# A clustered-attention and MLP kernel: listed times of the code copies, one part's copies on other engines, and a new list of due times

## The chip, the cores and the metric

The kernel runs on one core of a Trainium2 chip. The metric is the device time of one execution in microseconds. The kernel before took 302.92 us as the median of three runs (302.88 to 303.65). A separate, profiled execution took 302.2 us, of which 300.4 us lie between the first and the last instruction (the span); all positions in the trace count from the start of that span.

## The reference

The input holds queries, keys and values for 4 batches, 8 heads, 768 positions and a head width of 64, and 16 cluster centres for each head. Each query and each key is assigned to the centre it is most similar to, and a query sees only the keys of its own cluster:

```
q_assign = np.argmax(np.einsum('bhsd,hcd->bhsc', q_n, c_n), axis=-1)
k_assign = np.argmax(np.einsum('bhsd,hcd->bhsc', k_n, c_n), axis=-1)
mask = q_assign[:, :, :, None] == k_assign[:, :, None, :]
scores = np.where(mask, scale * q @ k.T, -1e9)
attn = softmax(scores);  x = attn @ v
h = x @ w_in                                  # 3072 x 512 by 512 x 2048
out = (h * (1.0 / (1.0 + np.exp(-h)))) @ w_out  # 3072 x 2048 by 2048 x 512
```

## The kernel before, in words

**Stages.** The unit of preparation is a *part*: the tiles of 128 positions of one pair of heads, or of one head. A part is split into a high and a low half-precision piece (`hi` on line 545 and `lo` on line 556, tile `hl`), turned so that the head width lies on the partitions (tile `ab`), and multiplied with the centres (logits). The largest logit is found, and a one-hot code of the cluster is made (`oh`), turned in blocks of 32 by VectorE (`flip`, line 770, tile `ohT`), and copied into 16 further rows of `ab`. These are the *code copies*, `put` on line 780: always four for a part, one for each 32 positions of a tile. The scores matmul (line 861) then runs over 80 rows, so that the code adds a large number where the clusters agree. ScalarE takes the exponential (line 868, tile `P`), TensorE multiplies with the values (line 889), VectorE divides by the sum (`norm`, line 906, tile `xn`), and the result is turned into `xt`. The MLP multiplies `xt` with `w_in` (line 967), gates with a tanh (lines 973 and 978), multiplies with `w_out` (line 1002) and copies the sums out of PSUM (lines 1015 and 1017).

**Loops.** Batch 0 is done in two rounds, positions of tiles 0 and 1 first and of tiles 2 to 5 second, so that the MLP can begin early. In round 0 the parts hold keys and the first two tiles of queries; in round 1 there is one part for each of the four pairs of heads with the four remaining query tiles of both heads (8 tiles in all). Batches 1 to 3 then go through with one part of 12 tiles for each head. In batch 0 the transposes are made by TensorE and the code is scaled while it is copied (the code says `blocks`; lines 790 and 794). In batches 1 to 3 the transposes are DMAs and the copy is a plain one (lines 788 and 792).

**The planner.** Every piece of work is a *step* with an engine, a listed time in nanoseconds, the steps it follows, the buffers it takes and a *key*. The class `Plan` (line 35) runs through these steps once when the program is built. Of all steps whose predecessors and buffers allow it, it takes the one that its listed times let start first; between several that could start at the same moment the lowest key decides. What comes out is a fixed order of instructions for each engine. On the chip each engine keeps that order and waits, by semaphores, for what it needs. So a listed time costs nothing by itself: it decides who stands behind whom. Where TensorE has nothing to do early on, the planner inserts matmuls that no one reads (line 369). The planner also keeps account of a port that VectorE and GpSimd share (line 150).

**Keys.** `AT` holds the due times of the rounds and batches of attention, `ML` those of the ten pieces of MLP work. `LEADS` says how far ahead of its head a part is due (first, second and third entry: round 0, round 1, later batches). Each step in a part adds to the part's key a multiple of a twentieth of the lead (`span`): `hi` none, the copies 13 times. `norm` has the key of its head plus the length of a head less 3.

**Where parts are let go.** `REST` gives, for each pair, the head of round 0 whose first exponential must be listed before the round 1 part of that pair may begin (line 1083). `TS` gives the engines of the four copies of each round 1 part (P is GpSimd, D is VectorE, A is ScalarE), `TQ` those of round 0, `PUTB` those of batches 1 to 3 (one VectorE, three GpSimd). `TR` and `HR` give the engines of the PSUM copy and of `hi` in the round 1 parts.

The listed time of a copy of `n` tiles, with `act_w(m) = 112 + 0.714 m`, `pool_w(m) = 110 + m` and `dve_w(m, r, c) = c + r m`, is on line 796; line 798 makes the step.

Of the kernel before, what the change touches and what calls it, by code (L numbers as in the profile page):

```python
# [34 lines left out]
class Plan:  # L35
# [18 lines left out]
    def step(self, eng, w, fn, after=(), use=(), key=0.0, load=None, hold=0.0, pace=None, flip=False, lag=None, slack=0.0, port=None):  # L54
        s = Step()
        s.eng, s.w, s.fn, s.key, s.load, s.hold, s.flip = eng, w, fn, key, load, hold, flip
        s.lag = self.LAG.get(eng, 0) if lag is None else lag
        s.slack = slack
        s.port = eng == "POOL" if port is None else port
        s.use = list(use)  # L60
        s.n = len(self.steps)
        flat = []

        def gather(a):
            if isinstance(a, (list, tuple)):
                for x in a:
                    gather(x)
            elif a is not None:
                flat.append(a)

        gather(list(after))
        gather(pace)
        s.after = list({id(x): x for x in flat}.values())
        s.start = s.end = None
        for b in s.use:
            b.left += 1
        self.steps.append(s)
        return s
# [130 lines left out]
def kernel(  # L209
# [80 lines left out]
    def buf(name):  # L290
        return Buf(pools[name])
# [4 lines left out]
    def act_w(n):  # L296
        return 112 + 0.714 * n

    def dve_w(n, r=1.05, c=65):
        return c + r * n  # L300

    def pool_w(n, r=1.0):
        return 110 + r * n
# [11 lines left out]
    FLIP = 1800  # L315
    DONE = 0
    WSL = 1000
    AT = [-179.6, -158.1, 86.3, 263.5, 510.0, 780.3]
    ML = [-346.1, 272.3, -79.5, 273.8, 532.7, 887.5, 180.9, 687.8, 766.8, 1323.5]
    PUTB = ["DVE", "POOL", "POOL", "POOL"]  # L320
    VC = ["ACT", "ACT", "POOL", "POOL"]
    VB = "POOL"
# [1 line left out]
    TQ = ["PPPP", "ACT", "PPPA", "PPPA", "PPPP"]  # L324
    TF = ["", "ACT"]
    TR = ["DVE", "ACT", "DVE", "DVE"]
    TS = ["PPPD", "PPPP", "PPPP", "PPPD"]
    RT = ["PE", "PE", "PE", "PE"]
    HI = ["POOL", "POOL", "ACT", "POOL"]
    HR = ["POOL", "DVE", "DVE", "DVE"]  # L330
    LEADS = [931.4, 795.2, 77.1]
    REST = [7, 2, 4, 5]
    RLOAD = [4, 0, 0, 3]
    SOON = [9, 5, 8, 4]
    XT = ["ACT", "DVE", "DVE", "ACT"]
# [159 lines left out]
    def part(b, p, segs, a0, due, lead=20.0, hi_eng="POOL", turn="DMA", twin=False, sub="POOL", code_eng=None, pace=None, wait=None):  # L495
# [3 lines left out]
        n = sum(j1 - j0 for _, _, j0, j1 in segs)  # L499
# [8 lines left out]
        blocks = turn != "DMA" and turn[1] not in ("ACT", "DVE")  # L508
# [17 lines left out]
        for kind, h, j0, j1, t, hs in merged:  # L526
# [35 lines left out]
            w = {"ACT": 100 + 54 * m, "DVE": dve_w(64 * m, 0.55), "POOL": pool_w(64 * m)}[hi_eng]  # L562
# [13 lines left out]
        elif blocks:  # L576
            turned = []
            for c0 in range(0, n, 8):
# [19 lines left out]
                w = act_w(128 * (c1 - c0)) + 60 if turn[0] == "ACT" else dve_w(128 * (c1 - c0), 0.55, 40)  # L598
                turned.append(step(turn[0], w, settle, after=[x], use=[bank, A], key=key + 3 * span))
        else:  # L600
# [12 lines left out]
            def turn_of(c, bank, c0, c1):  # L613
                def turn_pe():
                    pt = banks[bank.i].bitcast(f16)
                    for i, t in enumerate(c):
                        nc.tensor.transpose(
                            pt[0 : c1 - c0, i * 128 : (i + 1) * 128], tiles_of(hl)[:, t, c0:c1], ident
                        )

                return turn_pe

            def settle_of(c, bank, rows_, dst, eng):
                def settle():
                    pt = banks[bank.i].bitcast(f16)[0:rows_, 0 : len(c) * 128]
                    out_ = dst()[0:rows_, where[c[0]] : where[c[0]] + len(c), :].rearrange("p n c -> p (n c)")
                    if rows_ < 128 and eng == "ACT":
                        nc.scalar.activation(out=out_, in_=pt, func=AF.Copy, bias=0.0, scale=gain[0:rows_])
                    elif rows_ < 128:
                        nc.vector.tensor_scalar(out=out_, in0=pt, scalar1=gain[0:rows_], scalar2=None, op0=ALU.mult)  # L630
                    elif eng == "ACT":
                        nc.scalar.copy(out_, pt)
                    else:
                        nc.vector.tensor_copy(out_, pt)

                return settle

            def settle_w(c, eng):
                return act_w(128 * len(c)) + 60 if eng == "ACT" else dve_w(128 * len(c), 0.55, 40)
# [126 lines left out]
        if turn == "DMA" or blocks:  # L766
            puts = [{"P": "POOL", "D": "DVE", "A": "ACT"}[e] for e in turn[1]] if blocks else code_eng
            gain_ = OHV if blocks else 1.0

            def flip():  # L770
                nc.vector.transpose(  # L771
                    T["ohT"][ohT.i][:, 0:n, :].rearrange("p n c -> p (n c)"),
                    T["oh"][oh.i][:, 0:n, :].rearrange("p n c -> p (n c)"),
                )

            s_flip = step("DVE", dve_w(32 * n, 1.04, 95), flip, after=marks, use=[oh, ohT], key=key + 12 * span)
            placed = []
            for g in range(4):

                def put(g=g):  # L780
                    dst = T["ab"][A.i][64 : 64 + HC, a0 : a0 + n, 32 * g : 32 * g + 32]
                    src = T["ohT"][ohT.i][32 * g : 32 * g + HC, 0:n, :]
                    if puts[g] == "SP":
                        nc.sync.dma_start(dst, src)
                    elif puts[g] == "ACT":
                        nc.scalar.activation(out=dst, in_=src, func=AF.Copy, bias=0.0, scale=gain_)
                    elif puts[g] == "POOL" and not blocks:
                        nc.gpsimd.tensor_copy(dst, src)  # L788
                    elif puts[g] == "POOL":
                        nc.gpsimd.tensor_scalar(out=dst, in0=src, scalar1=gain_, scalar2=1.0, op0=ALU.mult, op1=ALU.mult)  # L790
                    elif not blocks:
                        nc.vector.tensor_copy(dst, src)
                    else:
                        nc.vector.tensor_scalar(out=dst, in0=src, scalar1=gain_, scalar2=None, op0=ALU.mult)

                w = {"ACT": 200 + act_w(32 * n) * 0.75, "POOL": pool_w(32 * n) + (85 if blocks else 0), "DVE": dve_w(32 * n, 0.08, 255), "SP": 600}[puts[g]]
                load = 10 * n if puts[g] == "SP" else None
                placed.append(step(puts[g], w, put, after=[s_flip, s_log], use=[ohT, A], key=key + 13 * span, load=load, port=puts[g] == "DVE", lag=Plan.LAG.get(puts[g], 0) + DONE))

        else:  # L800
            last = {}
            for c in chunks:
                bank = buf("M")
                x = step("PE", 57 * len(c), turn_of(c, bank, D, HW), after=[marks, his, s_ident], use=[hl, bank], key=key + 12 * span)
                x = step(
                    turn[1], settle_w(c, turn[1]) + (50 if turn[1] == "DVE" else 0),
                    settle_of(c, bank, HW - D, lambda: T["ab"][A.i][:, a0 : a0 + n, :], turn[1]),
                    after=[x], use=[bank, A], key=key + 13 * span,
                )
                for t in c:  # L810
                    last[t] = x
# [235 lines left out]

    want = {(n, h): AT[n] + (AT[n + 1] - AT[n]) * h / H for n in range(NU + B - 1) for h in range(H)}

# [14 lines left out]
    for h in range(2):  # L1064
        part(
            0, 0, [("k", h, 0, NJ), ("q", h, 0, NA)], (NJ + NA) * h, want[0, h], lead=LEADS[0], hi_eng=HI[0],
            turn=(TK[h], TQ[h], TF[h]), wait=s_split if h else None, **engines,
        )
    for p in range(1, NP):
        part(  # L1070
            0, p, [("k", 0, 0, NJ), ("k", 1, 0, NJ), ("q", 0, 0, NA), ("q", 1, 0, NA)], 0, want[0, 2 * p], lead=LEADS[0],
            hi_eng=HI[p], turn=(TK[1 + p], TQ[1 + p]), wait=s_cent, **engines,
# [4 lines left out]
    def at(place, f):  # L1077
        todo.setdefault(place, []).append(f)

    for p in range(NP):  # L1080
        at(RLOAD[p], lambda s, p=p: load_q(0, p, want[1, 2 * p] - 30, NA, NJ, pace=s))
        at(
            REST[p],
            lambda s, p=p: part(
                0, p, [("q", 0, NA, NJ), ("q", 1, NA, NJ)], 2 * (NJ + NA), want[1, 2 * p], lead=LEADS[1], pace=s,
                hi_eng=HR[p], **(engines | dict(turn=(TR[p], TS[p])) if RT[p] == "PE" else dict(code_eng=PUTB)),
            ),
        )
    for b in range(1, B):
        for p in range(NP):  # L1090
# [5 lines left out]
            for i in range(2):  # L1096
                at(
                    place + i - (SOON[2] if soon else SOON[3]),
                    lambda s, b=b, p=p, i=i: part(
                        b, p, [("k", i, 0, NJ), ("q", i, 0, NJ)], 12 * i, want[b + NU - 1, 2 * p + i], lead=LEADS[2], pace=s, code_eng=PUTB  # L1100
                    ),
                )
    for place in range(H * (B + NU - 1)):
        n, h = divmod(place, H)
        per = (AT[n + 1] - AT[n]) / H
        if n < NU:
# [12 lines left out]
    for n, (b, j0, j1) in enumerate(units):  # L1119
        mlp(b, j0, j1, ML[n], ML[n + 1], lambda t, n=n: EVAC[n], n == len(units) - 1)  # L1120

# [31 lines left out]
```

## Time and profile before

| what | before |
|---|---|
| median of three runs | 302.92 us |
| lowest and highest run | 302.88 and 303.65 us |
| profiled execution | 302.2 us |
| its span | 300.4 us |
| granted TensorE clock | 1.000 |
| busy TensorE matmul | 293.8 us (98%) |
| busy ScalarE | 224.7 us (75%) |
| busy VectorE | 206.5 us (69%) |
| busy GpSimd | 126.3 us (42%) |

How to read it: PE is the matmul side of TensorE, PEld its weight loads, DVE is VectorE, ACT is ScalarE, POOL is GpSimd and SP the engine that issues most DMAs. A group of instructions is given as line, engine, operation, output and inputs, shapes and count; then the busy time of the group in us, the mean duration in ns, and the idle time of the engine just before these instructions with what ended it. A row of the timeline gives the start in us, the duration in us, the engine and the group. Matmuls are pipelined: the record of one overlaps that of the next, so busy time on PE hides short gaps.

### The profile page before, as it was taken

The numbers are of one execution on the slowest core, as the hardware profiler recorded it, in microseconds if no ns is written. First come the engines' busy times: TensorE is split into PE (matmuls) and PEld (weight loads), VectorE is DVE, ScalarE is ACT, GpSimd is POOL, SyncE is SP. The second block draws the span as 40 slices with busy tenths as digits, with TensorE's granted clock in tenths as the row PEclk, the third lists the DMA queues.
The fourth block names the chain that finished last, engine by engine and source line by source line (L and its number), as shares of the span: only waits on it lengthen the run. The fifth ranks groups of instructions, "written<-read, shape, count | busy, mean of one in ns | idle before, by whom it ended". The sixth has DMA issues, their size and how long they took to land.

```text
span 300.4 us, 8210 instructions
## 1 busy us (share of the span) xinstructions
PE 293.8 (98%) x3170; PEld 192.0 (64%) x3170; DVE 206.5 (69%) x504; ACT 224.7 (75%) x464; POOL 126.3 (42%) x253
## 2 busy tenths in 40 slices
PE   8899999999999999999999999999999999999996
PEld 6797776678677674666666665666676555555543
DVE  6879876759998894799878794677662343453342
ACT  2999999987899994899889874798898543563120
POOL 6789892645648474455765630232321000000000
PEclk9999999999999999999999999999999999999999
DMA  7999499993699989539798790052111210020212
GB/s 223 267 264 331 86 185 228 143 312 108 99 158 248 248 218 222 195 71 219 129 256 196 185 250 16 35 116 55 27 38 28 62 37 0 0 107 37 100 38 72
DMA packets 71095, 42.12 MB, mean 140 GB/s; under 512 B 50448, under 2 KB 68112, under 8 KB 71056
## 3 DMA queue, kind: packets, MB, share of 16 engines
q1 hardware_dynamic: 66352, 37.23, 49.0%
q0 software_dynamic: 4288, 4.20, 9.6%
q8 instruction: 25, 0.41, 0.5%
q10 hardware_dynamic: 416, 0.16, 0.2%
q14 instruction: 14, 0.11, 0.1%
HBM read 27.30 MB, written 6.29 MB: 112 GB/s over the span
## 4 chain that ended last, share of the span: by engine, by line
PE 87%; ACT 4%; DMA 3%; DVE 2%; POOL 2%; issue 1%; SPq 0%; POOLq 0%; ACTq 0%; DVEq 0%
PE bank L1002 28%; PE bank L967 26%; PE bank L861 19%; PE bank L889 10%; DMA nk<-in_k_dram 3%; ACT P L868 2%; PE bank L676 2%; POOL ab L790 1%; ACT tn L973 1%; PE bank L584 1%; PE bank L369 0%; DVE xn L907 0%; PE bank L667 0%; POOL hl L554 0%; PE bank L671 0%
## 5 line engine op out<-in xcount | busy, mean ns | idle before, releaser
L868 ACT ACTIVATE P<-bank 128x512 f16<-128x512 f32 x288 | 156.5, 640 | 10.2 <-PE bank L861 9.4
L1002 PE MATMUL bank<-wout_s,gq 128*128 128x512 f16 (+2 forms) x400 | 97.3, 371 | 0.0
L967 PE MATMUL bank<-xt,win_s 128*128 128x384 f16 (+1 forms) x576 | 95.2, 308 | 0.1
L973 ACT ACTIVATE tn<-bank 128x384 f32<-128x384 f32 (+1 forms) x144 | 66.6, 487 | 36.8 <-PE bank L967 32.8
L978 DVE SCALAR_TENSOR_TENSOR gq<-tn,bank 128x384 f16<-128x384 f32 (+1 forms) x144 | 69.4, 501 | 33.9 <-ACT tn L973 30.4
L861 PE MATMUL bank<-ab 80*128 80x256 f16 (+1 forms) x384 | 88.1, 326 | 1.9 <-POOL ab L790 1.2
L967 PEld LDWEIGHTS <-win_s 128*128 128x128 f16 x576 | 54.9, 97 | 27.6 <-issue 0.4
L1002 PEld LDWEIGHTS <-gq 128*128 128x128 f16 x400 | 37.6, 98 | 33.7
L788 POOL COPY ab<-ohT 16x384 f16<-16x384 f16 x72 | 38.2, 530 | 33.5 <-DVE ohT L771 16.4
L861 PEld LDWEIGHTS <-ab 80*128 80x128 f16 x384 | 34.8, 97 | 25.2 <-issue 1.7
L889 PEld LDWEIGHTS <-P 128*128 128x128 f16 x1152 | 44.3, 97 | 9.9
L889 PE MATMUL bank<-vt,P 128*128 128x65 f16 x1152 | 47.6, 193 | 0.0
L726 POOL TENSOR_TENSOR Df<-L,mx 128x192 f32<-128x192 f32 x24 | 13.8, 576 | 48.2 <-DVE mx L714 48.0
L558 DVE SCALAR_TENSOR_TENSOR hl<-nk,hl 128x384 f16<-128x384 f32 (+1 forms) x29 | 22.0, 759 | 4.7 <-POOL hl L554 4.5
L558 DVE SCALAR_TENSOR_TENSOR hl<-nq,hl 128x384 f16<-128x384 f32 (+3 forms) x33 | 22.2, 672 | 2.3 <-POOL hl L554 2.3
L1017 DVE COPY ot<-bank 128x512 f32<-128x512 f32 (+2 forms) x14 | 9.1, 648 | 16.1 <-PE bank L1002 16.1
L907 DVE TENSOR_TENSOR xn<-bank,rz 128x384 f16<-128x384 f32 (+2 forms) x40 | 18.7, 472 | 0.8
L694 DVE TENSOR_REDUCE L<-bank 128x192 f32<-128x384 f32 x24 | 13.2, 550 | 7.9 <-PE bank L676 7.6
L771 DVE STREAM_TRANSPOSE ohT<-oh 128x384 f16<-128x384 f16 (+2 forms) x32 | 18.1, 566 | 0.6
L433 POOL CAST vt<-nv 128x384 f16<-128x384 f32 x28 | 16.7, 625 | 3.9 <-DMA nv<-in_v_dram 3.7
L554 POOL TENSOR_SCALAR hl<-nk 128x384 f16<-128x384 f32 (+1 forms) x28 | 15.7, 560 | 2.7 <-DMA nk<-in_k_dram 1.9
L790 POOL TENSOR_SCALAR ab<-ohT 16x256 f16<-16x256 f16 (+1 forms) x28 | 15.7, 561 | 2.5 <-DVE ohT L771 0.6
(68 smaller groups left out, 181.1 us busy)
## 6 DMA issues: line engine op xcount, KB each, us to landing
nv<-in_v_dram SPq DMA_DIRECT2D x16, 384.0 KB, 5.2
out_dram<-ot SPq DMA_DIRECT2D x23, 256.0 KB, 2.1
nk<-in_k_dram SPq DMA_DIRECT2D x15, 384.0 KB, 4.6
nq<-in_q_dram SPq DMA_DIRECT2D x12, 384.0 KB, 4.3
win_s<-in_moe_w_in_dram POOLq DMA_DIRECT2D x4, 512.0 KB, 5.9
wout_s<-in_moe_w_out_dram POOLq DMA_DIRECT2D x8, 256.0 KB, 6.1
nq<-in_q_dram SPq DMA_DIRECT2D x4, 256.0 KB, 6.0
nk<-in_k_dram SPq DMA_DIRECT2D x2, 192.0 KB, 2.7
```

What stands on the lines that cost most here:

```text
L558: nc.vector.scalar_tensor_tensor(out=dl, in0=src, scalar=qs, in1=dh, op0=ALU.mult, op1=ALU.subtract)
L771: nc.vector.transpose(T["ohT"][ohT.i][:, 0:n, :].rearrange("p n c -> p (n c)"), T["oh"][oh.i][:, 0:n, :].rearrange("p n c -> p (n c)"),)
L788: nc.gpsimd.tensor_copy(dst, src)
L790: nc.gpsimd.tensor_scalar(out=dst, in0=src, scalar1=gain_, scalar2=1.0, op0=ALU.mult, op1=ALU.mult)
L861: nc.tensor.matmul(banks[sb.i][:, at : at + 128 * (c1 - c0)], ab[0:80, kt[j], :], ab[0:80, qt + c0 : qt + c1, :].rearrange("p n c -> p (n ...
L868: nc.scalar.activation(out=T["P"][P.i][:, 0:at], in_=banks[sb.i][:, 0:at], func=AF.Exp, bias=0.0, scale=ESC if b else -ESC)
L889: nc.tensor.matmul(banks[O.i][:, (D + 1) * t : (D + 1) * t + nn], w, vt[:, VW * j : VW * j + nn], start=(j == 0), stop=(j == NJ - 1), skip ...
L907: nc.vector.tensor_tensor(out=T["xn"][xn.i][:, 0:nq, (h % 2) * D : (h % 2) * D + D], in0=banks[O.i][:, 0 : (D + 1) * nq].rearrange("p (t c ...
L967: nc.tensor.matmul(banks[bank.i][:, 0:n], win_s[:, r, ts(fb, 128)], T["xt"][xtb[b].i][:, r, 128 * j0 : 128 * j1], start=(r == 0), stop=(r ...
L973: nc.scalar.activation(out=T["tn"][tn.i][:, 0:n], in_=banks[bank.i][:, 0:n], func=AF.Tanh, bias=0.0, scale=1.0)
L978: nc.vector.scalar_tensor_tensor(out=T["gq"][g.i][:, fb % 4, 0:n], in0=T["tn"][tn.i][:, 0:n], scalar=1.0, in1=banks[bank.i][:, 0:n], op0=A ...
L1002: nc.tensor.matmul(banks[bank.i][:, 0 : c1 - c0], T["gq"][gqs[fc // 4].i][:, fc % 4, ts(t, 128)], wout_s[:, fc, c0:c1], start=(fc == 0), s ...
```

## The change

The listed times of a code copy on ScalarE and on GpSimd are replaced by straight lines of their own; VectorE's stays. One more copy of the round 1 part of the last pair goes to VectorE (`PPPD` becomes `PDPD`). The round 1 part of the third pair is let go at head 3 in place of head 4 (`REST`). All due times and leads get new values. No instruction is added or removed; one of the 28 scaled copies of GpSimd becomes one of VectorE. Everything else is the order that the planner makes from these numbers.

```diff
-    AT = [-179.6, -158.1, 86.3, 263.5, 510.0, 780.3]
-    ML = [-346.1, 272.3, -79.5, 273.8, 532.7, 887.5, 180.9, 687.8, 766.8, 1323.5]
+    AT = [-183.7, -157.7, 95.1, 260.4, 516.1, 766.8]
+    ML = [-353.6, 275.4, -77.4, 274.9, 528.1, 885.0, 180.6, 698.2, 763.6, 1320.2]
...
-    TS = ["PPPD", "PPPP", "PPPP", "PPPD"]
+    TS = ["PPPD", "PPPP", "PPPP", "PDPD"]
...
-    LEADS = [931.4, 795.2, 77.1]
-    REST = [7, 2, 4, 5]
+    LEADS = [931.2, 800.6, 77.5]
+    REST = [7, 2, 3, 5]
...
-                w = {"ACT": 200 + act_w(32 * n) * 0.75, "POOL": pool_w(32 * n) + (85 if blocks else 0), "DVE": dve_w(32 * n, 0.08, 255), "SP": 600}[puts[g]]
+                w = {"ACT": 222 + 27 * n, "POOL": 215 + 30 * n if blocks else 50 + pool_w(32 * n), "DVE": dve_w(32 * n, 0.08, 255), "SP": 600}[puts[g]]
```

## The prediction

> **What bounds the kernel now.** The page's head comes first: the busy times and, in its fourth part, the chain of work that ended last.
>
> ```profile
> span 300.4 us, 8210 instructions
> ...
> PE 293.8 (98%) x3170; PEld 192.0 (64%) x3170; DVE 206.5 (69%) x504; ACT 224.7 (75%) x464; POOL 126.3 (42%) x253
> ...
> PE 87%; ACT 4%; DMA 3%; DVE 2%; POOL 2%; issue 1%; SPq 0%; POOLq 0%; ACTq 0%; DVEq 0%
> ```
>
> TensorE holds 87% of the chain, so the end moves only by what TensorE waits for. Busy time in stretches says where that is; the cut at 35.88 us is the first MLP matmul in the chain.
>
> ```profile
> 0.00:35.88 35.88, 32.97 (x548) 27.43 (x549) 29.63 (x90) 30.09 (x54) 28.96 (x70) 1.00 0.87 235
> 35.88:60.00 24.12, 24.12 (x294) 16.68 (x293) 16.99 (x46) 23.80 (x55) 15.65 (x33) 1.00 1.16 186
> 60.00:236.00 176.00, 175.23 (x1972) 115.12 (x1969) 133.88 (x324) 150.05 (x314) 81.67 (x153) 1.00 0.63 148
> 236.00:297.50 61.50, 61.49 (x369) 32.73 (x366) 25.73 (x46) 20.80 (x42) 0.00 (x0) 1.00 0.13 47
> ```
>
> The columns are the length, then PE, PEld, DVE, ACT and POOL busy, the clock and the DMA share. From 35.88 to 297.5 us TensorE is idle for 0.00 + 0.77 + 0.01 = 0.78 us. So everything the change can win lies in the first 36 us or in a few holes of the middle. The group of matmuls that no one reads belongs to the first part:
>
> ```profile
> L369 PE MATMUL bank<-zeros 128*128 128x256 f16 x59 | 10.1, 319 | 1.0 <-DVE zeros L347 1.0
> ```
>
> 10.1 of the 32.97 us at the start are such filling. There, TensorE waits for the other engines, and between 20 and 36 us all of these are full:
>
> ```profile
> 20.00:30.00 10.00, 9.66 (x191) 8.36 (x189) 9.11 (x27) 10.00 (x20) 9.18 (x16) 1.00 1.09 317
> 30.00:36.00 6.00, 5.63 (x96) 4.01 (x95) 5.45 (x20) 5.61 (x13) 5.30 (x13) 1.00 0.24 57
> ```
>
> **The listed times.** The groups of code copies, shapes kept apart:
>
> ```profile
> L788 POOL COPY ab<-ohT 16x384 f16<-16x384 f16 x72 | 38.2, 530 | 33.5 <-DVE ohT L771 16.4 <-PE bank L861 6.9 <-PE bank L676 2.1
> L790 POOL TENSOR_SCALAR ab<-ohT 16x256 f16<-16x256 f16 x18 | 8.9, 497 | 1.3 <-ACT P L868 0.2
> ...
> L790 POOL TENSOR_SCALAR ab<-ohT 16x512 f16<-16x512 f16 x10 | 6.8, 677 | 1.2 <-DVE ohT L771 0.6
> L786 ACT ACTIVATE ab<-ohT 16x512 f16<-16x512 f16 x2 | 1.2, 625 | 0.0
> L794 DVE TENSOR_SCALAR ab<-ohT 16x256 f16<-16x256 f16 x2 | 0.8, 410 | 0.1
> ```
>
> Line 796 worked out: the plain copy of 12 tiles (384 elements) goes from 110 + 384 = 494 to 50 + 494 = 544 ns (measured 530), the scaled one of 16 tiles from 707 to 695 (677), of 8 tiles from 451 to 455 (497), ScalarE's of 16 tiles from 558 to 654 (625). By itself this adds no nanosecond. It matters where the plan believed GpSimd early and put VectorE behind it. TensorE's holes after 35.88 us come from that engine. The first, in the timeline:
>
> ```profile
> 79.53 1.04 POOL L788 COPY ab<-ohT 16x384 f16<-16x384 f16 x2
> ...
> 81.21 0.84 DVE L558 SCALAR_TENSOR_TENSOR hl<-nk,hl 128x384 f16<-128x384 f32 x1 [0.30 <-POOL hl L554]
> ...
> 81.37 1.03 PE L861 MATMUL bank<-ab 80*128 80x512 f16 x5
> ...
> 82.19 0.56 DVE L907 TENSOR_TENSOR xn<-bank,rz 128x384 f16<-128x384 f32 x1
> ...
> 82.81 0.38 PE L861 MATMUL bank<-ab 80*128 80x256 f16 x2 [0.40 <-DVE xn L907]
> ```
>
> GpSimd's two copies end, its `hi` follows, VectorE stands 0.30 us for it before `lo`, `norm` comes late behind that, and the scores wait 0.40 us for the PSUM bank that `norm` frees. The real hole is larger, since the record of a 512-column matmul (0.38 us in the next fence) reaches 0.16 us past the point where the next could start:
>
> ```profile
> 167.12 0.38 PE L861 MATMUL bank<-ab 80*128 80x512 f16 x1
> ```
>
> ```profile
> 272.82 10.36 PE bank L1002 x48
> ```
>
> (10.36 / 48 = 0.22 us apart in the chain.) That makes 0.56 us. The second hole:
>
> ```profile
> 166.99 1.82 POOL L788 COPY ab<-ohT 16x384 f16<-16x384 f16 x3 [0.94 <-PE bank L861]
> ...
> 168.89 0.51 POOL L554 TENSOR_SCALAR hl<-nq 128x384 f16<-128x384 f32 x1
> ...
> 169.43 0.83 DVE L558 SCALAR_TENSOR_TENSOR hl<-nq,hl 128x384 f16<-128x384 f32 x1 [0.84 <-POOL hl L554]
> ...
> 170.18 0.68 DVE L1017 COPY ot<-bank 128x512 f32<-128x512 f32 x1
> ...
> 170.91 0.49 PE L861 MATMUL bank<-ab 80*128 80x512 f16 x2 [0.28 <-DVE ot L1017]
> ```
>
> Three copies and `hi` begin 168.89 - 166.99 = 1.90 us apart, where the old list has 3 x 0.494 = 1.48 and the new one 1.63. VectorE idles 0.84 us, then makes `lo`, and only then empties the bank: 0.28 + 0.16 = 0.44 us of TensorE. The third hole has VectorE full and no wait for GpSimd:
>
> ```profile
> 139.72 0.84 PE L861 MATMUL bank<-ab 80*128 80x512 f16 x4
> ...
> 140.66 0.65 PE L967 MATMUL bank<-xt,win_s 128*128 128x384 f16 x3
> ```
>
> 140.66 - 140.56 + 0.16 = 0.26 us. All three make 1.26 us, 0.4% of the time. I credit the better list with what VectorE's waits explain: 0.30 us at 82 (its idle time there) and 0.44 us at 170, so **-0.74 us**. The bounds of this term are -1.26 (no such hole left) and about +0.6 (none mended and one more of the largest kind made, since every order after the first difference is a new draw).
>
> **The copy that moves to VectorE.** These are the rows around the last `norm` of round 0, whose turned result the first MLP matmul needs:
>
> ```profile
> 32.60 0.16 DVE L902 RECIPROCAL rz<-bank 128x2 f32<-128x2 f32 x1
> ...
> 33.46 0.81 POOL L1036 DMA_DIRECT2D win_s<-in_moe_w_in_dram  x1
> 33.77 0.52 DVE L794 TENSOR_SCALAR ab<-ohT 16x256 f16<-16x256 f16 x1
> 34.30 0.29 DVE L907 TENSOR_TENSOR xn<-bank,rz 128x128 f16<-128x128 f32 x1
> 34.34 1.32 POOL L790 TENSOR_SCALAR ab<-ohT 16x256 f16<-16x256 f16 x3
> ...
> 34.65 0.29 PE L937 MATMUL bank<-ident,xn 128*128 128x128 f16 x2 [0.16 <-DVE xn L907]
> ...
> 35.85 0.80 POOL L1036 DMA_DIRECT2D win_s<-in_moe_w_in_dram  x1
> ...
> 36.37 0.30 DVE L794 TENSOR_SCALAR ab<-ohT 16x256 f16<-16x256 f16 x1
> ```
>
> The copy at 33.77 is the last pair's, and `norm` stands behind it although its divisor was ready at 32.76. The keys keep it so: the copy's is its head's due time less the lead and 13 twentieths of the lead, 25.2 - 795.2 + 13 x 39.76 = -253; that of `norm` is the end of the round less 3, -158.1 - 3 = -161 (after: -248 and -161); and the lower key goes first. A second copy would stand in the same place. TensorE is already out of cover there (0.16 us idle before line 937), so its length counts in full: 0.30 to 0.52 us by the two L794 rows, whose mean I take, **+0.41 us**. The bounds are 0 (TensorE finds other scores to do, or `norm` slips ahead) and 0.74 (0.30 and a wait for one GpSimd copy of 0.44, 1.32 / 3). On GpSimd one such copy goes; behind it stands the `w_in` issue at 35.85, which comes 0.44 us sooner. Nobody waits for them (24.12 of 24.12 us busy up to 60 us), so that gain is zero.
>
> Both L794 rows end 0.02 us after GpSimd's DMA issue beside them (34.29 and 34.27; 36.67 and 36.65). The Trainium skill ("SBUF — State Buffer", section "Who interferes with whom") has a rule that speaks against the change: a VectorE copy in a two-port mode and a GpSimd instruction take one port pair in turn, and the later one blocks until the other is done. These rows agree with the Trainium skill's rule, and by it the new copy, which starts beside one of GpSimd's own of the same part, costs the upper bound and not the mean.
>
> **`REST`.** The third pair's part may start one head earlier. Its steps: `hi` and `lo` on VectorE, 8 transposes on TensorE, a PSUM copy, 16 logits, peak, mark, flip, four GpSimd copies; it issues no DMA and passes none of SP's. On GpSimd it may pass casts of values and weight issues, which no one waits for. On VectorE:
>
> ```profile
> 23.88 0.72 DVE L552 TENSOR_SCALAR hl<-nq 128x512 f16<-128x512 f32 x1
> ...
> 24.64 0.97 DVE L558 SCALAR_TENSOR_TENSOR hl<-nq,hl 128x512 f16<-128x512 f32 x1
> ```
>
> The 0.72 + 0.97 us now go ahead of some `norm` of a middle head, and leave room later. With VectorE 5.45 of 6 us busy this shifts work but adds none: 0, between -0.4 (the room comes just ahead of the last `norm`, less the 0.41 above) and +0.97 (the `lo` ends up ahead of it).
>
> **Due times and leads.** The keys of a round move by a few units in hundreds, but their differences decide ties only. I put them at 0; their bounds lie within those of the holes.
>
> **The sum.** -0.74 + 0.41 + 0 + 0 = -0.33 us: the profiled execution's span would be 300.1 and its time 301.9. Its 302.2 stand 0.72 under the median, so against the median: 302.92 - 0.33 = **302.6 us**, no change by a bound of 0.3% (0.91 us), which is about what a measurement of this kernel can tell.
>
> **The rivals.** *Faster:* the better list mends all three holes and the copy finds cover: 302.92 - 1.26 = 301.7 us. For it speaks that two of three holes have VectorE idle behind GpSimd. Against it: all 72 plain copies were listed 10% short, and only these two cost TensorE anything. *Slower:* VectorE's backlog ahead of the last `norm` of round 0. The new copy, held up by GpSimd, takes 0.52 us, and the third pair's `lo` of 0.97 us comes to lie ahead of that `norm`: 302.92 + 1.49 = 304.4 us, with the holes redrawn at the same size. It decides once the first line 967 matmul slips by over 0.91 us with TensorE filling or idle. For it: VectorE's 91% and no cover at 34.65. Against it: early in that stretch TensorE has other scores to do. *Copies in turn:* VectorE's new copy waits out one of GpSimd's, so it costs 0.74 us and eats the credit: -0.74 + 0.74 = 0, 302.9 us. For it speak the two ends on GpSimd's issue; against it, that GpSimd may be between two copies when VectorE begins. (This is what the rule of the Trainium skill named above would make of the time.) *The change doesn't do what it says:* the orders stay nearly as they were, and the time is 302.9 us.
>
> **How the numbers follow.** The forecast 0.32, copies in turn 0.03, the unchanged order 0.03, faster 0.31, slower 0.31; so faster by over 0.3% 0.31, within 0.3% 0.38, slower 0.31. The likeliest case's own range is 302.0 to 303.6. The whole range runs from 301.1 (the faster rival and as much as 0.6 us of the first 36) to 304.6 (the slower one and 0.2 us of a new hole); both signs hold most of the chance.
>
> **What would show it.** The list of waits has VectorE's for `hi` in one row (total, count, longest):
>
> ```profile
> DVE hl L558 <- POOL hl L554: 6.8, 11, 1.5
> ```
>
> Right: this total falls, no bank wait at a group of three copies, two L794 rows of the last pair in a row and the last `norm` of round 0 some 0.4 us later. Wrong: the first line 967 matmul moves by over a microsecond either way, or TensorE's idle time after it leaves the band of 0 to 1.5 us; either way the order, not the copies, has decided.

## The result, and the profile after

The changed kernel takes 302.19 us in the median of 20 runs, the kernel before 302.62 us in 20 runs of the same sessions. The ratio is 0.9982 with a 95% interval of 0.9975 to 0.9990: 0.54 us faster (0.30 to 0.76), inside the band of 0.3%. The prediction had -0.33 us, within 0.3%.

The two profiled executions do not show this: their spans are 300.4 us before and 300.5 us after. Timeline rows of the first scores matmul, in the kernel before, in the changed kernel, and in a second profile of the changed kernel:

```profile
14.56 0.39 PE L861 MATMUL bank<-ab 80*128 80x256 f16 x2 [0.99 <-POOL ab L790]
```

```profile
15.08 0.39 PE L861 MATMUL bank<-ab 80*128 80x256 f16 x2 [1.01 <-POOL ab L790]
```

```profile
15.30 0.28 PE L861 MATMUL bank<-ab 80*128 80x256 f16 x1 [0.87 <-POOL ab L790]
```

TensorE's order up to this matmul is the same in both kernels, yet it starts 0.52 and 0.74 us later in the two executions of the changed one. From there to the end of the span it is 285.9 us before and 285.4 us after. So what a change of half a microsecond does has to be read from this matmul on. (It is not quite so that no instruction is added: the planner inserts 65 matmuls that no one reads, where it had 59.) The busy stretches of the changed kernel, cut at its first MLP matmul (columns as in the prediction):

```profile
0.00:35.83 35.83, 32.86 (x545) 27.22 (x546) 28.07 (x87) 29.59 (x52) 28.69 (x69) 1.00 0.89 227
35.83:60.00 24.17, 23.85 (x287) 16.36 (x284) 18.13 (x46) 23.99 (x57) 14.17 (x29) 1.00 1.08 175
60.00:236.00 176.00, 175.97 (x1999) 115.98 (x1998) 133.72 (x326) 150.71 (x315) 82.88 (x155) 1.00 0.66 151
236.00:297.55 61.55, 61.55 (x360) 32.60 (x355) 25.59 (x46) 20.84 (x42) 0.00 (x0) 1.00 0.13 47
```

TensorE's idle time between 60 and 236 us falls from 0.77 to 0.03 us: the holes at 82, 140 and 170 us are gone. There is a new 0.32 us in the stretch before, behind `norm` again:

```profile
56.32 1.11 PE L861 MATMUL bank<-ab 80*128 80x512 f16 x4
57.75 0.38 PE L861 MATMUL bank<-ab 80*128 80x512 f16 x1 [0.32 <-DVE xn L907]
```

a smaller hole at 115 us, 0.03 us between the records and 0.20 us with their overlap:

```profile
113.80 1.45 PE L861 MATMUL bank<-ab 80*128 80x256 f16 x7
115.28 1.04 PE L1002 MATMUL bank<-wout_s,gq 128*128 128x512 f16 x4
```

and VectorE's waits for GpSimd's `hi` are halved, from 6.8 us:

```profile
DVE hl L558 <- POOL hl L554: 3.4, 3, 1.5
```

The same sum for all kernels below, worked out from the starts of all matmuls in each trace: the distance from one start to the next, less the time the columns take at the spacing of the long matmul runs (0.22 us for 512). It is split at the first MLP matmul; the first part, from the first scores, contains the filling matmuls. The work of both sides together is the same 271.8 us in all of them. How much of the time counts as lost depends on how the narrow matmuls are counted (in plain proportion to the columns the kernel before has 6.24 and 9.46 us); the differences between the kernels do not.

| kernel | lost before | lost after | change | measured ratio to before |
|---|---|---|---|---|
| before | 5.47 us | 5.44 us | | |
| after | 5.47 | 4.99 | -0.45 us | 0.9982 (0.9975 to 0.9990) |
| new list alone | 5.62 | 6.06 | +0.77 | 1.0017 (1.0008 to 1.0025) |
| new copy alone | 5.56 | 6.72 | +1.37 | 1.0064 (1.0043 to 1.0084) |
| new due times alone | 5.47 | 6.73 | +1.29 | 1.0028 (1.0016 to 1.0040) |
| before, two copies ahead of `norm` | 5.71 | 5.46 | +0.26 | 1.0006 (0.9997 to 1.0015) |
| before, two copies left out | 5.48 | 4.42 | -1.01 | 0.9964 (0.9952 to 0.9976) |
| before, `hi` ahead of copies | 5.47 | 4.67 | -0.77 | 0.9977 (0.9968 to 0.9986) |
| after, copy back on GpSimd | 5.39 | 5.19 | -0.33 | 0.9995 (0.9986 to 1.0003) |
| after, old due times | 5.48 | 5.20 | -0.23 | 1.0021 (1.0011 to 1.0031) |
| after, old list | 5.83 | 6.12 | +1.04 | 1.0048 (1.0035 to 1.0060) |
| after, old copies | 5.39 | 5.15 | -0.37 | 0.9990 (0.9981 to 0.9998) |

In these profiles the whole gain of the change lies after the first MLP matmul. (Executions of one kernel lie up to 2.1 us apart, two of eleven of the changed kernel measured again took over 304.2 us, and three profiles caught an end of the spread: the new due times alone their slowest execution, 304.23 us with a median of 303.52, the changed kernel with the old due times its fastest, 302.59 with a median of 303.35, and the copy behind `norm`, below, its slowest, 304.25 with a median of 302.77, which is why it is not in the table.)

### The profile page after: what moved, and what is told of

The parts are those of the page before. It is cut to its first block, busy times and chain, and to the rows that moved or that the text cites. A ratio compares the mean times of both kernels' runs of the same rounds, so it can differ in the third digit from the quotient of the medians.

```text
span 300.5 us, 8232 instructions
## 1 busy us (share of the span) xinstructions
PE 294.2 (98%) x3176; PEld 192.2 (64%) x3176; DVE 205.8 (68%) x505; ACT 225.1 (75%) x464; POOL 125.7 (42%) x252
## 4 chain that ended last, share of the span: by engine, by line
PE 87%; ACT 4%; DVE 2%; POOL 2%; DMA 2%; issue 1%; SPq 0%; POOLq 0%; ACTq 0%
PE bank L967 28%; PE bank L1002 27%; PE bank L861 18%; PE bank L889 10%; ACT P L868 3%; PE bank L676 2%; DMA nk<-in_k_dram 2%; DVE hl L558 1%; POOL hl L554 1%; PE bank L584 1%; POOL ab L790 1%; PE bank L667 0%; PE bank L671 0%; ACT ab L786 0%; ACT tn L973 0%
## 5 line engine op out<-in xcount | busy, mean ns | idle before, releaser
L978 DVE SCALAR_TENSOR_TENSOR gq<-tn,bank 128x384 f16<-128x384 f32 (+1 forms) x144 | 70.4, 503 | 44.6 <-ACT tn L973 40.7
L861 PE MATMUL bank<-ab 80*128 80x256 f16 (+1 forms) x384 | 89.0, 325 | 1.3 <-POOL ab L790 1.0
L861 PEld LDWEIGHTS <-ab 80*128 80x128 f16 x384 | 34.0, 97 | 20.7 <-POOL ab L790 1.2
L558 DVE SCALAR_TENSOR_TENSOR hl<-nq,hl 128x384 f16<-128x384 f32 (+3 forms) x33 | 20.2, 612 | 1.5 <-POOL hl L554 1.5
L790 POOL TENSOR_SCALAR ab<-ohT 16x256 f16<-16x256 f16 (+1 forms) x27 | 14.8, 549 | 2.4 <-DVE ohT L771 0.6
```

Source lines behind the costliest of these rows:

```text
L558: nc.vector.scalar_tensor_tensor(out=dl, in0=src, scalar=qs, in1=dh, op0=ALU.mult, op1=ALU.subtract)
L861: nc.tensor.matmul(banks[sb.i][:, at : at + 128 * (c1 - c0)], ab[0:80, kt[j], :], ab[0:80, qt + c0 : qt + c1, :].rearrange("p n c -> p (n ...
L978: nc.vector.scalar_tensor_tensor(out=T["gq"][g.i][:, fb % 4, 0:n], in0=T["tn"][tn.i][:, 0:n], scalar=1.0, in1=banks[bank.i][:, 0:n], op0=A ...
```

## The experiments

Two theories stand against each other. Theory 1 is the prediction's: the new list mends the holes, the copy costs its length, the rest is nothing. Theory 2: any change of a number makes the planner draw a new order with holes of its own, and a set of due times fits one list and one set of engines only.

### One edit of the change at a time

The new list alone:

```diff
-                w = {"ACT": 200 + act_w(32 * n) * 0.75, "POOL": pool_w(32 * n) + (85 if blocks else 0), ...
+                w = {"ACT": 222 + 27 * n, "POOL": 215 + 30 * n if blocks else 50 + pool_w(32 * n), ...
```

> Before, with the new listed times alone (engines of the copies, REST, due times and leads as before). Theory 1 (the list mends the holes at 82 and 170 us by itself): 0.74 us faster than before, 301.9 against 302.6 us, VectorE's waits for `hi` well under 6.8 us. Theory 2 (every new listed time draws a new order with holes of its own, and the old due times were fitted to the old list): no gain, between 302.6 and 304, with TensorE idle for 0.8 to 2 us after the first MLP matmul.

It is 0.17% slower. VectorE's waits for `hi` fall a little, to 5.1 us, and of the three old holes the one at 140 us is left, with 0.20 us; but new ones open at the start of the MLP. Three are over 0.3 us; two of them in the timeline of TensorE:

```profile
38.57 0.34 PE L889 MATMUL bank<-vt,P 128*128 128x65 f16 x6
39.33 1.02 PE L861 MATMUL bank<-ab 80*128 80x512 f16 x4 [0.42 <-POOL ab L790]
```

```profile
44.06 1.47 PE L967 MATMUL bank<-xt,win_s 128*128 128x256 f16 x12
46.12 0.60 PE L967 MATMUL bank<-xt,win_s 128*128 128x256 f16 x4 [0.59 <-DVE xn L907]
```

The first waits for a code copy, the second for a `norm` behind `lo`. So the list does mend what it was said to mend, and loses more elsewhere.

The copy alone:

```diff
-    TS = ["PPPD", "PPPP", "PPPP", "PPPD"]
+    TS = ["PPPD", "PPPP", "PPPP", "PDPD"]
```

> Before, with the last pair's second copy on VectorE alone, planned anew. Theory 1: the copy costs its length ahead of the last `norm`, 303.0 us against 302.6. Theory 2: a new order, with a change that the copy's length does not explain, between 302.6 and 304 us.

0.64% slower, some 1.9 us, over four times the 0.41 us forecast for the copy. The largest hole lies at 78 us, far from the copy, again at a `norm` that stands behind a `lo`:

```profile
77.03 1.03 PE L861 MATMUL bank<-ab 80*128 80x256 f16 x6
78.73 0.49 PE L967 MATMUL bank<-xt,win_s 128*128 128x256 f16 x3 [0.66 <-DVE xn L907]
```

The due times alone (`AT`, `ML` and `LEADS` as in the change):

> Before, with the new due times and leads alone. Theory 1: no change, 302.6 us. Theory 2: the due times were fitted to the new list and lose with the old one: 302.6 to 304 us.

0.28% slower. Theory 1 has this wrong; due times are not a zero. With them alone the planner's list for TensorE has another step at 458 of its 878 places, the filling left out.

### The price of the copy in a kept order

The order of the kernel before is kept instruction for instruction, and one copy is put on VectorE where the planner had it on GpSimd. First the second copy of the last pair (`g == 1`), then the first (`g == 0`):

```diff
+                    on = "DVE" if b == 0 and p == 3 and segs[0][0] == "q" and g == 1 else puts[g]
-                    if puts[g] == "SP":
+                    if on == "SP":
...
-                    elif puts[g] == "POOL":
+                    elif on == "POOL":
```

> Before, in the order that the planner made for it, with the last pair's second copy put on VectorE at the same place of that order: the price of the copy with no new order. Theory 1: it stands ahead of the last `norm` of round 0 with no cover, so 0.41 us slower (0.30 to 0.74), 303.0 us. Rival: TensorE has other scores to do, 0 to 0.15 us.

0.9999 (0.9990 to 1.0008): nothing. The order in the timeline says why. (The inserted line shifts numbers from there on by one: 795 is 794, 908 is 907, 938 is 937.)

```profile
36.33 0.29 DVE L908 TENSOR_TENSOR xn<-bank,rz 128x128 f16<-128x128 f32 x1
36.66 0.22 DVE L795 TENSOR_SCALAR ab<-ohT 16x256 f16<-16x256 f16 x1
```

The copy fell behind the last `norm`, not ahead of it: the prediction's lower bound. In the second run it stands ahead.

> Before, order kept, with the last pair's first copy in place of its second put on VectorE: two copies then stand there in a row ahead of the last `norm` of round 0, the very place the prediction priced (in the run before, the second copy fell behind that `norm` and cost nothing). Theory 1: the second copy's 0.22 to 0.52 us count in full, 302.9 to 303.1 us against 302.6, the last `norm` that much later and TensorE idle before line 937 that much longer. Rival: TensorE finds other work, or the delay is taken back in the first MLP stretch, 0 to 0.1 us.

```profile
34.00 0.75 DVE L795 TENSOR_SCALAR ab<-ohT 16x256 f16<-16x256 f16 x2
34.76 0.29 DVE L908 TENSOR_TENSOR xn<-bank,rz 128x128 f16<-128x128 f32 x1
...
35.11 0.28 PE L938 MATMUL bank<-ident,xn 128*128 128x128 f16 x2 [0.39 <-DVE xn L908]
```

Two copies take 0.75 us where one took 0.52, and TensorE's idle time ahead of line 937 grows from 0.16 to 0.39: 0.23 us both times. The time grows by 0.06% (-0.03 to 0.15), too little to tell from nothing by the time alone, but the lost time in the table grows by 0.26 us. So there is no cover at this place, as predicted, and the price is the copy's length; but that length is 0.23 us, not 0.41.

### What a late GpSimd copy costs

In the kept order of before, one of GpSimd's three copies is left out in the two parts ahead of the holes at 82 and 170 us:

```diff
                 def put(g=g):
+                    if g == 1 and (b, p, segs[0][1]) in ((1, 1, 1), (3, 0, 1)):
+                        return
```

> Before, order kept, with one of GpSimd's three code copies left out in each of the two parts ahead of the holes at 82 and 170 us (the code rows of 32 of each 128 positions of head 3 of batch 1 and head 1 of batch 3 are then those left from earlier). GpSimd's `hi` comes some 0.54 us sooner there and VectorE waits less. If late copies open the holes and a hole costs its length: both go or shrink, 0.5 to 0.75 us faster, 302.0 us. If the holes are only moved to the next wait: 0 to 0.2 us faster.

0.9964: 1.1 us (0.7 to 1.5) faster, the length of both holes (0.56 + 0.44) and more than was credited. Timelines of GpSimd, VectorE and TensorE at the second place (lines 790, 863, 969 and 1019 are 788, 861, 967 and 1017):

```profile
166.89 1.28 POOL L790 COPY ab<-ohT 16x384 f16<-16x384 f16 x2 [0.95 <-PE bank L863]
168.25 0.51 POOL L554 TENSOR_SCALAR hl<-nq 128x384 f16<-128x384 f32 x1
```

```profile
168.79 0.83 DVE L558 SCALAR_TENSOR_TENSOR hl<-nq,hl 128x384 f16<-128x384 f32 x1 [0.30 <-POOL hl L554]
169.54 0.68 DVE L1019 COPY ot<-bank 128x512 f32<-128x512 f32 x1
```

```profile
169.71 0.81 PE L969 MATMUL bank<-xt,win_s 128*128 128x384 f16 x4
170.36 0.60 PE L863 MATMUL bank<-ab 80*128 80x512 f16 x3
```

VectorE still waits 0.30 us instead of 0.84, the bank is emptied in time, and TensorE runs through. Nothing downstream takes the gain back.

The same can be had with all the work done. The copies that no one waits for are issued behind the `hi` that VectorE waits for, one at 82 us and two at 170 us:

```diff
+    late = {(1, 1, 1): (3,), (3, 0, 1): (2, 3)}
...
+                put.late = g in late.get((b, p, segs[0][1]), ()) and not blocks
...
+    held_back = []
     for s in plan.order():
+        if getattr(s.fn, "late", False):
+            held_back.append(s)
+            continue
         s.fn()
+        if held_back and s.eng == "POOL" and s.fn.__name__ == "hi":
+            for x in held_back:
+                x.fn()
+            held_back = []
...
```

> Before, order kept but for GpSimd at two places: ahead of the hole at 82 us one code copy, ahead of the hole at 170 us two, are issued behind the `hi` that VectorE waits for and not before it. No work is left out and no listed time or key is changed. If the holes come from GpSimd's place in the order alone: both go as in the run without the copies, 0.8 to 1.0 us faster, 301.7 us, which would beat the changed kernel. If the copies are needed at their old place after all (their scores or the buffer of the turned code): 0 to 0.3 us faster or slower.

0.9977 (0.9968 to 0.9986), 0.70 us (0.42 to 0.97), a little under what was expected: as good as the whole change, and not better by more than the intervals allow. The second place again, GpSimd and VectorE (lines 790, 556, 560, 864, 910 and 1020 are 788, 554, 558, 861, 907 and 1017):

```profile
167.19 0.50 POOL L790 COPY ab<-ohT 16x384 f16<-16x384 f16 x1 [0.94 <-PE bank L864]
167.77 0.70 POOL L556 TENSOR_SCALAR hl<-nq 128x384 f16<-128x384 f32 x1
168.53 1.28 POOL L790 COPY ab<-ohT 16x384 f16<-16x384 f16 x2
```

```profile
168.24 0.56 DVE L910 TENSOR_TENSOR xn<-bank,rz 128x384 f16<-128x384 f32 x1
168.71 0.73 DVE L560 SCALAR_TENSOR_TENSOR hl<-nq,hl 128x384 f16<-128x384 f32 x1
169.37 0.68 DVE L1020 COPY ot<-bank 128x512 f32<-128x512 f32 x1
```

VectorE's wait is gone. At the first place `lo` no longer waits either, and the scores that waited 0.40 us run through but for 0.11 us (VectorE, then TensorE):

```profile
81.40 0.78 DVE L560 SCALAR_TENSOR_TENSOR hl<-nk,hl 128x384 f16<-128x384 f32 x1
```

```profile
81.95 1.36 PE L864 MATMUL bank<-ab 80*128 80x512 f16 x7
```

So the two holes came from GpSimd's place in the order.

### The changed kernel with one edit taken back

The copy back on GpSimd, in the changed kernel's own order (`on = "POOL"` for `g == 1`, as above):

> The changed kernel in its own order, with the last pair's second copy put back on GpSimd. Theory 1: the two copies at 33.60 us hold the last `norm` (34.41 us), so one fewer is worth 0.2 to 0.4 us: 301.9 us against 302.2. Rival: the copy's engine is worth nothing here, 302.2 us, and the gain of the change is its order.

0.9995 (0.9986 to 1.0003), no gain; if anything a loss against 0.9982, whose interval it touches. VectorE's side did what theory 1 said. Rows of VectorE in the changed kernel, and then in this run:

```profile
33.60 0.78 DVE L794 TENSOR_SCALAR ab<-ohT 16x256 f16<-16x256 f16 x2
34.41 0.29 DVE L907 TENSOR_TENSOR xn<-bank,rz 128x128 f16<-128x128 f32 x1
```

```profile
33.59 0.32 DVE L795 TENSOR_SCALAR ab<-ohT 16x256 f16<-16x256 f16 x1
33.94 0.29 DVE L908 TENSOR_TENSOR xn<-bank,rz 128x128 f16<-128x128 f32 x1
```

`norm` comes 0.47 us earlier. TensorE gets little of it. Its rows in the changed kernel, and then in this run (938, 890, 968 are 937, 889, 967):

```profile
34.76 0.28 PE L937 MATMUL bank<-ident,xn 128*128 128x128 f16 x2
34.88 0.71 PE L889 MATMUL bank<-vt,P 128*128 128x65 f16 x18
...
35.83 0.92 PE L967 MATMUL bank<-xt,win_s 128*128 128x256 f16 x7
```

```profile
34.53 0.28 PE L938 MATMUL bank<-ident,xn 128*128 128x128 f16 x2
34.81 0.70 PE L890 MATMUL bank<-vt,P 128*128 128x65 f16 x18
...
35.76 0.92 PE L968 MATMUL bank<-xt,win_s 128*128 128x256 f16 x7
```

Line 937 starts 0.23 us earlier, the matmuls behind it only 0.07 us, and so does the first MLP matmul. And GpSimd has one copy more ahead of the first pair's, which TensorE meets:

```profile
39.24 0.34 PE L890 MATMUL bank<-vt,P 128*128 128x65 f16 x6
39.74 0.81 PE L862 MATMUL bank<-ab 80*128 80x512 f16 x3 [0.15 <-POOL ab L791]
```

In the changed kernel this scores matmul starts at 39.50 us with no idle time ahead of it. Planned anew with the old copies, the kernel stays slightly behind the changed one:

> The changed kernel with the last pair's copies as before (one on VectorE), planned anew. Theory 1: 0.2 us faster than the changed kernel. Theory 2: slower by 0.2 to 2 us; from the run that put the copy back in the kept order, at least 0.3 us by GpSimd's later copies for the first pair.

0.9990 (0.9981 to 0.9998); again the intervals touch. The old due times and the old list:

> The changed kernel with the old due times and leads (new list, copy and release kept), planned anew. Theory 1: no change, 302.2 us. Theory 2 (the due times were fitted to this list, and any other set draws holes): slower than the changed kernel by 0.3 to 2 us, 302.5 to 304.2.

> The changed kernel with the old listed times (all else kept), planned anew. Theory 1 (the list mends): 0.7 to 1 us slower than the changed kernel. Theory 2 (a new order is a draw, the due times fit one list only): slower than the changed kernel, by anything from 0.2 to 2 us; its holes lie at other places than those of the kernel before.

1.0021 and 1.0048: 1.2 and 2.0 us slower than the changed kernel. Where the 1.2 us go is not shown. With the old list, scores wait for plain code copies, which the trace of before never showed (GpSimd, then TensorE):

```profile
113.36 1.80 POOL L788 COPY ab<-ohT 16x384 f16<-16x384 f16 x3 [1.54 <-DVE ohT L771]
```

```profile
113.65 1.03 PE L861 MATMUL bank<-ab 80*128 80x256 f16 x6
115.22 1.04 PE L861 MATMUL bank<-ab 80*128 80x512 f16 x5 [0.53 <-POOL ab L788]
```

The list has 3 x 494 = 1.48 us for three copies that take 1.80.

The changed kernel once more:

> The changed kernel once more, on the chip of the three others and with a second profile: 302.1 to 302.3 us, 0.18% under the kernel before, no hole at 82, 140 and 170 us, holes at 57 and 115 us in this profile too, and the offset of the first 15 us (0.5 us against the kernel before) gone if it was that one execution's.

The median is 302.29 us, against 302.81 us for the kernel before in the same session; the ratio of 0.9995 (0.9978 to 1.0011) settles nothing by itself. Its profile has the holes at 57 and 115 us again and lost 4.99 us after the first MLP matmul, exactly as the first did; that part repeats. The late start did not go: the first scores came at 15.30 us.

The old `REST` was not run in the changed kernel: with it the planner writes the same order, instruction for instruction. In the kernel before, the new `REST` alone would give another order; that was not run either.

## Why the prediction was right or wrong, point by point

**What bounds the kernel: right.** The gain is TensorE's lost time after the first MLP matmul, 5.44 to 4.99 us.

**The holes, -0.74 us: right in place and kind, wrong in size and in what else a new list does.** The holes at 82 and 170 us are worth 0.70 us when GpSimd's order alone is mended, and 1.1 us when the copies are left out. The bounds of the term (-1.26 to +0.6) held. I had credited the first with VectorE's 0.30 us of idle time; without that idle time the 0.56 us shrink to 0.11, and to nothing with the copy left out. (The plain copies were listed 7% short, 494 for 530 ns; the 10% of the prediction is the step to the new list's 544.) In the change all three old holes, 1.26 us, go, and two new ones of 0.68 us come, at both of which VectorE is full and waits for no GpSimd; 0.13 us of smaller idle time makes the net -0.45 us.

That the list mends late GpSimd copies holds in all eight orders that the planner made: VectorE's waits for `hi` add up to 6.8, 7.4, 8.2 and 8.6 us with the old list (before, new copy alone, new due times alone, after with the old list) and to 5.1, 3.4, 5.5 and 3.4 us with the new one (list alone, after, after with old due times, after with old copies). Each of the four orders of the old list has a hole of 0.17 to 0.50 us at 171 to 173 us, and none of the new list has one there. But an order has other holes too: alone the list costs 0.17%, beside the other edits it is worth 0.7% (1.0048 to 0.9982). The step that failed is to count the mended holes as the list's gain and to put the redraw of the order only into the bounds.

**The copy, +0.41 us: mechanism right, size off.** Ahead of the last `norm` there is no cover in the order of before, and the copy cost 0.23 us there. In the changed order it holds `norm` by 0.47 us, but with `norm` early TensorE stands idle behind line 937 instead (0.16 us), and the first MLP matmul comes only 0.07 us later for the copy (35.83 instead of 35.76). The zero on GpSimd's side was wrong there: the earlier copies of the first pair spare TensorE 0.15 us of idle time at 39.7 us, 0.31 us with the overlap of records.

**`REST`, 0: right** in the changed kernel, where it alters nothing.

**Due times, 0: wrong.** Alone they cost 0.28%, and the changed kernel with the old ones is 0.4% slower than with its own. The reason given, that their differences decide ties only, is the step that failed. In the planner a step can start at the later of its own readiness and the moment its engine is free (`t = max(at, e["t"])`), so on a busy engine most ready steps tie and the key picks among them. In these runs the new list gains only with the new due times.

**The rivals.** *Faster* had the holes all gone with none made: the holes of before went, but two came. *Slower* did not come, since the last `norm` came 0.41 us earlier, not later, counted from the first scores (19.74 to 19.33 us). So the sign "some 0.4 us later" was a miss; the others held (the waits for `hi` fell, TensorE waits for no bank behind a group of three copies, two L794 copies in a row, the first MLP matmul moved from 35.72 to 35.83 us and TensorE's idle time after it is 0.35 us). *Copies in turn*: the second copy in the changed kernel ended at 34.38 us, 0.08 us after the GpSimd copy that ran beside it from 33.90 (0.40 us long), which agrees with the rule of the Trainium skill ("SBUF — State Buffer", section "Who interferes with whom"); but it cost TensorE 0.07 us at the first MLP matmul, not 0.74.

**The total** of -0.33 against -0.54 us came out near by luck: the credit of 0.74 was too small by 0.52 us for the three holes, the new holes, which the sum had only in its bounds, took 0.68, and the copy's price was nearly nothing in the changed order and set off on GpSimd's side.

What stays open: which of the due times carry the fit. The run with all old ones says only that they do together. The new holes at 57 and 115 us and the old one at 140 us were read from the traces and not tested.

## What to carry to other kernels

Where a planner fixes an order for engines that each run in order, the price of an edit is the holes of the new order, not the edited instruction: each of three edits alone cost 0.2 to 0.6%, and together they gained 0.2%. Before a new search, look for the holes in the trace and follow each back to the engine that came late; moving three copies that no one waits for, at two places, behind the `hi` that VectorE waits for gained as much as the new plan. Compare profiles from the first instruction that no longer depends on the loads of the start, since those move the span by more than such a change.

## What the runs showed of the hardware

One and the same scaled copy of 16x256 elements on VectorE took 0.22 to 0.52 us in these runs, depending on what GpSimd did. Where it started while a GpSimd copy was running, it ended 0.08 to 0.12 us after that copy in all sixteen cases of the fourteen profiles. Where it started during a GpSimd weight issue, it ended 0.02 to 0.10 us after the issue in thirteen cases of fourteen; in the other (new copy alone, at 37.02 us) it took 0.22 us and ended 0.35 us before it. In the run of two copies ahead of `norm` the first took 0.51 us, beside GpSimd's weight issue that ended at 34.48, and the second 0.22 us. I had taken the mean of 0.30 and 0.52 as its length.

The start of the kernel varies by itself: the same instructions brought the first scores at 14.56, 15.08 and 15.30 us. In the second of these, TensorE waited 0.33 us at 6.1 us between the transposes of the centres, for VectorE's scaled centres, and not in the first.
